# Moving v's copies, two matmul fillers, one group's normalisation and the last value units, and turning a third of batch 4's q by DMA, in a windowed-attention and gated-MLP kernel

## The chip, the cores and the metric

One core of one Trainium2 chip. The metric is device time in microseconds (us) for one execution of the whole program; the time of a kernel is the median of its runs.

## The reference

Sliding-window causal attention (window 64) over q, k, v of 8 batches, 8 heads, 576 positions and head size 64, and on its output, seen as 4608 tokens of 512 features, a two-layer MLP with the gate h·cos(h):

```python
scores = 1/sqrt(64) * q @ k^T                 # per batch and head
mask   = 0 <= query - key < 64
attn   = softmax(where(mask, scores, -1e9))
x      = (attn @ v) as (B*S, H*D)             # 4608 x 512
h      = x @ w_in                             # 512 -> 2048
out    = (h * cos(h)) @ w_out                 # 2048 -> 512, float32
```

## The kernel before, in words

**Units and groups.** Queries are cut into blocks of 64 positions (j = 0 to 8 in each batch) and heads into pairs p = 0 to 3. A *unit* is one (batch, pair, block): a 128 x 128 score tile that holds two heads over 64 queries, and the 128 keys that the window can reach. Two to four units make a *group*, which passes through the engines as one: scores on PE (`g_scores`), masked maximum on DVE (`g_max`), exponential with row sums on ACT (`g_exp`), reciprocal of the sums on DVE (`g_inv`), multiplication on POOL into the bf16 weights w (`g_norm`; a few on DVE), and a transposition of the weights (`g_trans`): by a DMA that SyncE's queue SP issues ("wT<-w"), or for a few "direct" groups by PE, with a copy on DVE (`g_put`). Then `values` multiplies the turned weights with v on PE, eight units for each pair, and `put_x` copies the result from PSUM into xT.

Groups are numbered: 0 to 7 are blocks 0 to 7 of batch 0 and 8 its block 8. Of batch 1, group 9 + 2p has blocks 0 to 3 of pair p, 10 + 2p blocks 4 to 6, and 17 and 18 the rest. `n_listed` is 19, so groups 19 to 28 are batch 2: 19, 20, 22, 23 are blocks 0 to 3 of one pair each, 21 has blocks 4 and 5 of pairs 0 and 1, and 24, the sixth, those of pairs 2 and 3; 25 to 28 have blocks 6 to 8. Batch 3 has six groups of 3, 3, 4, 3, 3, 4 units for blocks 0 to 4, and four of 4 units for blocks 5 to 8.

**v.** v's rows are loaded 128 to a chunk into every other slot of a tile. A block's keys may straddle two chunks, so the odd slots are filled by copies within the tile, one for each half of the partitions (`spread_v`): by a DMA from SP, or by POOL or DVE.

**q and k.** From batch 2 on they arrive in six chunks of 96 positions. k's chunks are turned by DMA transposes from SP (`turn_k`). q is turned by PE, six small transposes for each pair (`tr_q`), which DVE copies into the block layout qB (`put_block`). For the batches named in `TURNED`, the first 2 chunks (batches 5 and 6), or all 6 (batch 7), are turned by DMA instead (`turn_q`), and two DVE copies put them in place (`put_turned`).

**The MLP.** Tokens are taken in tiles of 512 (mt = 0 to 8). In one tile's stage PE does 64 matmuls with w_in (line 440), ACT takes the sine of each of the 16 results, DVE multiplies (gT, line 579), and PE does 64 matmuls with w_out (line 590). The scores of the next batch are placed among the second 64, and at the end of the stage come the next tile's values (line 371).

**What sets the order.** The program of each engine is in the order in which the Python code emits it. Up to the values of mt = 1 that is written out by hand in `FIRST` (a list of short codes: `Gn.13.p` is `g_norm` of group 13 on POOL, `y.0.s` is v's copy of batch 1, half 0, by SP, `Gc` a DMA transposition of weights, `V.2` the values of pair 2). After that, steps are entered with planned times (`at`) and emitted by `pump` as the matmuls pass these times; T = 32 is a stage in plan time. An engine runs its instructions in order and waits at the first that is not ready, so a step placed earlier or later on one queue (SP's and POOL's among them) moves all that stands behind it.

Of the kernel before, what the change touches and what calls it, by code (L numbers as in the profile page):

```python
# [10 lines left out]
def _safe_warn(msg, *a, **kw):  # L11
# [3 lines left out]
F32 = mybir.dt.float32  # L15
# [9 lines left out]
NC, NP = 6, 96  # L25
GF = 4
# [11 lines left out]
PAIRS = 4  # L38
Q = 16
T = 2 * Q  # L40
# [1 line left out]
SKEW = 3  # L42
DIRECT = (0, 7, 8)
OUTS = 3
TURNED = {5: 2, 6: 2, 7: 6}

# [24 lines left out]
)  # L71


# [1 line left out]
def kernel(  # L75
# [9 lines left out]
    nc = tc.nc  # L85
    B, H, S, D = q.shape
# [5 lines left out]
    MT = 512  # L92
    TU = MT // 64
# [8 lines left out]
    ps_t = ctx.enter_context(tc.tile_pool(name="ps_t", bufs=3, space=PSUM))  # L102
# [13 lines left out]
    ident = const.tile([128, 128], BF16, name="ident")  # L116
# [5 lines left out]
    st = {}  # L122
# [9 lines left out]
    def bank(which, name):  # L132
        return ps.tile([128, 512], F32, tag=which, name=name)
# [57 lines left out]
    def spread_v(b, half, engine="p", lo=0, hi=4):  # L191
        vt = vtiles[b % 2]
        hi = min(hi, 4 - (half == 0))
        d = slice(64 * half, 64 * half + 64)
        of = 2 * lo + 2 * (half == 0)
        to, of = vt[d, 2 * lo + 1:2 * hi:2], vt[d, of:of + 2 * (hi - lo) - 1:2]
        if engine == "s":
            nc.sync.dma_start(out=to, in_=of)
        else:
            copy(engine, to, of)  # L200
# [80 lines left out]
    def g_scores(n, which):  # L281
        s_ps = bank((BANKS if n < n_listed else S_BANKS)[which], "s_ps")
        units = groups[n]
        s_ps = s_ps[:, 0:len(units) * 128].rearrange("p (u c) -> p u c", c=128)
        if n < n_first:
            m0 = 2 if units[0][2] else 0
            for h in range(2):
                d = slice(64 * h, 64 * h + 64)
                nc.tensor.matmul(out=s_ps[d].rearrange("p u c -> p (u c)"), lhsT=ident[d, d],
                                 rhs=mask16[d, m0:m0 + len(units)].rearrange("p u c -> p (u c)"),  # L290
                                 start=True, stop=False, skip_group_check=True)
        for u, (b, p, j) in enumerate(units):
            kt = st["kT", b, p]
            lo = max(64 * j - 64, 0)
            rhs = kt[:, lo:lo + 128].rearrange("d (a t) -> d a t", a=2)
            if j and j % 2 == 0:
                rhs = rhs[:, ::-1, :]
            if b > 1:
                nc.tensor.matmul(out=s_ps[:, u].rearrange("p (a t) -> p a t", a=2),  # L299
                                 lhsT=qblocks[(b % 2) * PAIRS + p][:, j].rearrange("d h t -> d (h t)"), rhs=rhs,  # L300
                                 start=True, stop=True, skip_group_check=True)
                continue
            for h in range(2):
                d = slice(64 * h, 64 * h + 64)
                nc.tensor.matmul(out=s_ps[d, u].rearrange("p (a t) -> p a t", a=2),  # L305
                                 lhsT=qtiles[b * PAIRS + p][d, 64 * j:64 * j + 64], rhs=rhs[d], start=n >= n_first,
                                 stop=n >= n_first or u == len(units) - 1, skip_group_check=True)
        st["s", n] = s_ps
# [39 lines left out]
    def g_trans(n):  # L348
        w, u = st.pop(("w", n)), len(groups[n])
        if n in direct:  # L350
            st["tw", n] = t_ps = ps_t.tile([128, GF, 128], BF16, tag="t", name="tw_ps")
            for i in range(u):
                nc.tensor.transpose(t_ps[:, i], w[:, i], ident)
            return
        wT = att.tile([128, GF, 128], BF16, tag="wT", name="wT", bufs=20)
        nc.sync.dma_start(out=wT[:, 0:u], in_=w[:, 0:u].rearrange("p u c -> p (u c)"), transpose=True)
        st.update({("wT", unit): wT[:, i] for i, unit in enumerate(groups[n])})
# [4 lines left out]
        st.update({("wT", unit): wT[:, i] for i, unit in enumerate(groups[n])})  # L362


    def values(mt, p):
        st["o", mt, p] = o_ps = bank("S", "o_ps") if mt > 1 and p == PAIRS - 1 else ps_t.tile([128, MT], F32, tag="t", name="o_ps")
        for i in range(TU):
            b, j = divmod(mt * TU + i, NU)
            wT = st["wT", (b, p, j)]
            for h in range(2):  # L370
                nc.tensor.matmul(out=o_ps[64 * h:64 * h + 64, 64 * i:64 * i + 64],  # L371
                                 lhsT=vtiles[b % 2][:, max(j - 1, 0), 128 * p + 64 * h:128 * p + 64 * h + 64],
                                 rhs=wT[:, 64 * h:64 * h + 64], start=True, stop=True, skip_group_check=True)
# [90 lines left out]
    def at(time, fn, *args):  # L464
        plan.append((time, len(plan), fn, args))
# [10 lines left out]
    n = n_listed  # L476
    for t in range(1, B - 1):
        last = max(i for i, units in enumerate(groups) if units[0][0] == t + 1)
        time = T * t + Q - 1.4
        for i in range(last + 1 - n):  # L480
            time += PACE * len(groups[n - 1]) if i else 0
            at(time, g_scores, n, i % 3)
            lags = LAGS[:2] + tuple(T * t + T - 0.79 - time + 0.01 * s for s in range(3)) if n == last else LAGS
            for lag, fn in zip(lags, (g_max, g_exp, g_inv, g_norm)):
                at(time + lag, fn, n)
            at(time + (4.6 if n in direct else lags[-1]), g_trans, n)
            if n in direct:
                at(time + 4.9, g_put, n)
            ready.update({unit: time + (5.9 if n in direct else 8.5) for unit in groups[n]})
            n += 1  # L490

    for b in range(2, B):
        t0 = T * (b - 1)
        for h in range(2):
            if b in TURNED:
                at(t0 + 0.6 + 0.5 * h, put_turned, b, h, 0, 3)
            if TURNED.get(b, 0) > 2:
                at(t0 + (11 + h if TURNED[b] == NC else 10 + 0.5 * h), put_turned, b, h, 3, TURNED[b] * NP // 64)
        for c in range(TURNED.get(b, 0)):
            at(t0 - T + (23.4 if c < 2 else 26.4) + 0.01 * c, turn_q, b, c)  # L500
        for p in range(PAIRS if TURNED.get(b) != NC else 0):
            t_q = t0 + (2 if b == 2 else 1) + (3.3 if b == 2 else 3.5) * p
            for lag, fn, *args in ((0, tr_q), (0.02, put_block, 0), (0.5, put_block, 1)):
                at(t_q + lag, fn, b, p, *args)
        if b > 2:
            for c in range(NC):
                for i, name in enumerate(("q", "k")):
                    at(t0 - T + 5.6 + 1.6 * c + 0.8 * i, load_chunk, name, b, c)
        for c in range(NC):
            at(t0 + (2 + 1.2 * c if b == 2 else (-5.4, -5.3, -5.2, -4, -2.5, -1.5)[c] if TURNED.get(b) == NC else c - 5.5),  # L510
               turn_k, b, c)
        for c in range(5):
            at(t0 + 0.5 + c, load_v, b, c)
        for half_ in range(2):
            at(t0 + (22.2 + 0.1 * half_ if b > 2 else 10), spread_v, b, half_, "p" if b > 2 else "s")
    for mt in range(2, n_mt):
        for p in range(PAIRS):
            time = T * mt - (8.01 if mt == n_mt - 1 else 1.01)
            at(time, values, mt, p)
            at(time + (0.2 if p < 2 else 0.2 + 0.1 * p), put_x, mt, p, "a" if p == 2 else None)  # L520


# [7 lines left out]
    def spread_first(lo, hi):  # L530
        return lambda i, engine: spread_v(0, i, engine, lo, hi)
# [10 lines left out]
             "pq": lambda p, engine: put_q(0, p, engine), "pk": lambda p, engine: put_k(0, p, engine),  # L542
             "Pq": lambda p, engine: put_q(1, p, engine), "Pk": lambda p, engine: put_k(1, p, engine),
             "zA": spread_first(0, 1), "zB": spread_first(1, 3), "zC": lambda engine: spread_v(0, 1, engine, 3, 4),
             "y": lambda half_, engine: spread_v(1, half_, engine),
             "s": lambda p, g, which: g_scores(2 * p + g, which), "m": lambda p, g: g_max(2 * p + g),
             "e": lambda p, g: g_exp(2 * p + g), "i": lambda p, g: g_inv(2 * p + g),
# [82 lines left out]
```

## Time and profile before

| | us |
|---|---|
| runs shown | 518.71, 310.45, 311.47 |
| their median | 311.47 |
| the profiled execution | 311.39 |
| its span on the core | 309.6 |

| engine | busy us | share of the span |
|---|---|---|
| PE (TensorE matmul) | 295.6 | 95% |
| ACT (ScalarE) | 235.8 | 76% |
| DVE (VectorE) | 229.1 | 74% |
| POOL (GpSimd) | 191.9 | 62% |

The profile is of one execution. All times in its views count from the start of its span. A row of a timeline gives start, length, engine, source line, operation, "out<-in" by tile names, how many instructions it merges, and in brackets the idle time of the engine before it with what ended it. A row of the chain of waits gives start, length and what was on the chain. A row of the windows gives the window, its length, and the busy time of each engine with its instruction count, then the granted TensorE clock.

### The profile page before, as it was taken

Reading aid. Unit: us, or ns where it says so; the run is one execution under the profiler, and the core shown is the slowest. Engines: PE = TensorE matmul, PEld = TensorE weight load, DVE = VectorE, ACT = ScalarE, POOL = GpSimd, SP = SyncE. Lnnn points to the kernel's source line nnn. Section 1 sums busy time; section 2 is a strip of 40 time slices with the busy share of each in tenths; the row PEclk is TensorE's granted clock in tenths of the full one; section 3 lists DMA queues with packets and bytes.
Section 4 is the critical chain, followed back from the end, with each engine's and each line's share of the span. In section 5 each row is a group of like instructions: output and inputs, shape, how many; then the busy total and the mean of one; then the engine's idle time right before and its main releaser. Section 6 shows DMA issues by size and latency. Waiting matters only on the chain.

```text
span 309.6 us, 7899 instructions
## 1 busy us (share of the span) xinstructions
PE 295.6 (95%) x2587; PEld 160.3 (52%) x2619; DVE 229.1 (74%) x877; ACT 235.8 (76%) x785; POOL 191.9 (62%) x227
## 2 busy tenths in 40 slices
PE   3889999899999999999999999999999999999996
PEld 3768844445545455455454555455545554454443
DVE  5998988589767986798679876987598758335801
ACT  4998799577997699769976998699869986116600
POOL 8998577993569659966997699858902840000000
PEclk9999999999999999999999999999999999999999
DMA  8999999999949993999999999999993834011011
GB/s 151 179 214 186 200 178 136 132 156 177 242 81 126 143 235 68 105 125 228 146 97 121 193 191 92 149 173 192 120 134 78 197 70 152 2 68 71 0 65 71
DMA packets 159321, 42.14 MB, mean 136 GB/s; under 512 B 147440, under 2 KB 154544, under 8 KB 159280
## 3 DMA queue, kind: packets, MB, share of 16 engines
q0 software_dynamic: 100192, 18.06, 82.6%
q1 hardware_dynamic: 58944, 23.38, 42.0%
q8 instruction: 20, 0.33, 0.5%
q14 instruction: 21, 0.17, 0.2%
q10 hardware_dynamic: 144, 0.20, 0.2%
HBM read 36.70 MB, written 9.44 MB: 149 GB/s over the span
## 4 chain that ended last, share of the span: by engine, by line
PE 77%; DMA 8%; DVE 5%; POOL 3%; ACT 3%; issue 2%; POOLq 0%; DVEq 0%; ACTq 0%
PE h_ps L440 31%; PE out_ps L590 30%; PE h_ps L404 4%; DMA w_in<-in_moe_w_in_dram 3%; PE s_ps L299 3%; DVE gT L579 3%; DMA wT<-w 3%; PE out_ps L423 3%; PE o_ps L371 3%; ACT e L330 3%; DMA q<-in_q_dram 2%; POOL w L344 1%; POOL v L187 1%; PE out_ps L452 1%; PE tq_ps L218 1%
## 5 line engine op out<-in xcount | busy, mean ns | idle before, releaser
L590 PE MATMUL out_ps<-w_out,gT 128*128 128x512 bf16 x482 | 115.3, 379 | 0.8 <-issue 0.2
L440 PE MATMUL h_ps<-xT,w_in 128*128 128x512 bf16 x498 | 114.6, 379 | 1.0
L330 ACT ACTIVATE e<-s,negm 128x128 f32<-128x128 f32 x256 | 98.6, 388 | 0.6 <-DVE negm L319 0.6
L576 ACT ACTIVATE sin<-h_ps 128x512 f32<-128x512 f32 x128 | 73.8, 598 | 33.1 <-PE h_ps L440 31.0
L579 DVE TENSOR_TENSOR gT<-h_ps,sin 128x512 bf16<-128x512 f32 x128 | 82.0, 685 | 22.2 <-ACT sin L576 21.5
L344 POOL TENSOR_TENSOR w<-e,rden 128x512 bf16<-128x512 f32 (+1 forms) x75 | 71.2, 965 | 37.5 <-DVE rden L337 36.3
L440 PEld LDWEIGHTS <-w_in 128*128 128x128 bf16 x512 | 48.8, 98 | 54.7 <-issue 0.4
L590 PEld LDWEIGHTS <-gT 128*128 128x128 bf16 x496 | 46.0, 98 | 44.1
L319 DVE CUSTOM_DVE_ANT_0 s<-s_ps,mask 128x128 f32<-128x128 f32 x256 | 58.5, 286 | 1.3 <-PE s_ps L305 1.0
L330 ACT ACTIVATION_READ_ACCUMULATOR e<-s,negm 128x1 f32 x256 | 48.2, 188 | 0.0
L181 POOL DMA_DIRECT2D k<-in_k_dram x36 | 28.3, 788 | 9.9 <-DMA k<-in_k_dram 7.8
L187 POOL DMA_DIRECT2D v<-in_v_dram x40 | 34.3, 875 | 0.2 <-issue 0.2
L181 POOL DMA_DIRECT2D q<-in_q_dram x36 | 28.6, 794 | 7.1 <-DMA v<-in_v_dram 2.5
L337 DVE RECIPROCAL rden<-den 128x4 f32<-128x4 f32 (+1 forms) x79 | 13.7, 173 | 21.0 <-ACT e L330 18.0
L136 ACT COPY out_sb<-out_ps 128x512 f32<-128x512 f32 (+1 forms) x18 | 10.2, 565 | 24.5 <-PE out_ps L590 18.4
L299 PEld LDWEIGHTS <-qB 128*128 128x128 bf16 x216 | 17.1, 98 | 14.2
L136 DVE CAST xT<-o_ps 128x512 bf16<-128x512 f32 x24 | 15.6, 679 | 10.6 <-PE o_ps L371 10.5
L136 DVE COPY out_sb<-out_ps 128x512 f32<-128x512 f32 x18 | 12.4, 689 | 12.9 <-PE out_ps L590 12.4
L299 PE MATMUL s_ps<-kT,qB 128*128 128x128 bf16 x216 | 21.9, 219 | 0.0
L319 DVE DVE_READ_ACCUMULATOR2_ANT negm<- 128x1 f32 x256 | 21.3, 83 | 0.0
L136 POOL COPY v<-v 64x1536 bf16<-64x1536 bf16 (+1 forms) x10 | 16.8, 1676 | 0.3
L136 DVE COPY qB<-tq_ps 64x576 bf16<-64x576 bf16 (+1 forms) x40 | 16.4, 410 | 0.3
(65 smaller groups left out, 253.6 us busy)
## 6 DMA issues: line engine op xcount, KB each, us to landing
out_dram<-out_sb SPq DMA_DIRECT2D x16, 512.0 KB, 7.6
v<-in_v_dram POOLq DMA_DIRECT2D x32, 128.0 KB, 5.8
q<-in_q_dram POOLq DMA_DIRECT2D x36, 96.0 KB, 8.6
k<-in_k_dram POOLq DMA_DIRECT2D x36, 96.0 KB, 8.6
w_in<-in_moe_w_in_dram POOLq DMA_DIRECT2D x4, 512.0 KB, 9.6
w_out<-in_moe_w_out_dram POOLq DMA_DIRECT2D x4, 512.0 KB, 10.9
wT<-w SPq DMA_TRANSPOSE x68, 4.4
q<-in_q_dram POOLq DMA_DIRECT2D x7, 144.0 KB, 5.5
```

The costliest lines, as they stand in the source:

```text
L136: {"a": nc.scalar.copy, "p": nc.gpsimd.tensor_copy}.get(engine, nc.vector.tensor_copy)(out, in_)
L181: nc.gpsimd.dma_start(out=st[name, b][:, c].rearrange("p (h d) -> p h d", h=H), in_=src.rearrange("h p d -> p h d"))
L187: nc.gpsimd.dma_start(out=vt.rearrange("p (h d) -> p h d", h=H), in_=v[b, :, c * 128:c * 128 + n, :].rearrange("h p d -> p h d"))
L299: nc.tensor.matmul(out=s_ps[:, u].rearrange("p (a t) -> p a t", a=2), lhsT=qblocks[(b % 2) * PAIRS + p][:, j].rearrange("d h t -> d (h t)" ...
L319: nc.vector.tensor_tensor_reduce(out=s[:, u], in0=s_ps[:, u], in1=mask[:, 2 - j % 2 if j else 0], scale=-scale if b else -1.0, scalar=BIG, ...
L330: nc.scalar.activation(e[:, u], s[:, u], AF.Exp, bias=negm[:, u:u + 1], scale=1.0 if n < n_first else -1.0, accum_out=den[:, u:u + 1])
L337: nc.vector.reciprocal(out=rden[:, 0:len(groups[n])], in_=den[:, 0:len(groups[n])])
L344: (nc.gpsimd if engine == "p" else nc.vector).tensor_tensor(out=w[:, 0:u], in0=e[:, 0:u], op=ALU.mult, in1=rden[:, 0:u].unsqueeze(2).to_br ...
L440: nc.tensor.matmul(out=st["h", ff], lhsT=w_in_sb[:, ks, ff * 128:ff * 128 + 128], rhs=st["xT", mt][:, ks], start=start, stop=stop)
L576: nc.scalar.activation(sin, h_ps, AF.Sin, bias=math.pi / 2.0)
L579: nc.vector.tensor_tensor(out=gt[:, e], in0=h_ps, in1=sin, op=ALU.mult)
L590: nc.tensor.matmul(out=o_ps[e], lhsT=gT[ff // 2][:, ff % 2, ms * 128:ms * 128 + 128], rhs=w_out_sb[:, ff], start=ff == 0, stop=ff == n_ff - 1)
```

## The change

- `TURNED` gains batch 4 with 2 chunks: SP issues two DMA transposes of q in the stage before, planned at 24.3 (the other batches have 23.4), which puts them behind the sixth weights of batch 3 on SP's queue. PE's transposes for batch 4 go from 24 to 16; DVE's eight copies from `tr_q` take 6 of 9 blocks each, and two copies from the turned tile are added.
- In `FIRST` v's copy of batch 1, half 0, leaves SP (`y.0.s`, one DMA of 64 x 3 x 512). POOL does it in two parts: `yA.p` (2 x 512) behind the weights of group 14, `yB.p` (512) behind those of group 13.
- Group 24's multiplication goes from POOL to DVE.
- Fillers on PE: one 128 x 512 matmul of the mask ahead of group 12's scores, and four 128 x 128 transposes of the identity ahead of group 6's. Their results are written over.
- v's POOL copies for batch 3 are planned at 24 instead of 22.2. On POOL they move from behind the fourth of batch 3's ten multiplications to behind the sixth.
- For mt = 2 and 3, the values of pairs 2 and 3 are emitted in two steps: units 0 to 5 of both, then units 6 and 7 of both.
- The loads of batch 7's v are planned 7.5 later. On POOL's queue their order is the same as before.

```diff
+FILL = (6, 12)
-TURNED = {5: 2, 6: 2, 7: 6}
+TURNED = {4: 2, 5: 2, 6: 2, 7: 6}
...
-    "Gi.14 Gm.15 Gs.17.1 oc.1.d Gc.9 y.0.s Gn.11.p Gi.13 Gm.16 o.1.2 Ge.8 Ge.16 Ge.15 y.1.d Gn.14.p Gi.8 "
-    "Gc.12 Gm.17 o.0.3.0 Gi.16 Gn.13.p Gc.11 Gn.8.p Lq2.3 Lq2.4 Lq2.5 o.2.2 Gn.16.d Gw.8 Gc.14 Gc.13 "
...
+    "Gi.14 Gm.15 Gs.17.1 oc.1.d Gc.9 Gn.11.p Gi.13 Gm.16 o.1.2 Ge.8 Ge.16 Ge.15 y.1.d Gn.14.p yA.p Gi.8 "
+    "Gc.12 Gm.17 o.0.3.0 Gi.16 Gn.13.p yB.p Gc.11 Gn.8.p Lq2.3 Lq2.4 Lq2.5 o.2.2 Gn.16.d Gw.8 Gc.14 "
...
     def g_scores(n, which):
         s_ps = bank((BANKS if n < n_listed else S_BANKS)[which], "s_ps")
         units = groups[n]
+        if n == FILL[1]:
+            nc.tensor.matmul(out=s_ps, lhsT=ident, rhs=mask16[:, 0:4].rearrange("p u c -> p (u c)"), start=True, stop=True,
+                             skip_group_check=True)
...
             st["tw", n] = t_ps = ps_t.tile([128, GF, 128], BF16, tag="t", name="tw_ps")
+            for i in range(GF if n == FILL[0] else 0):
+                nc.tensor.transpose(t_ps[:, i], ident, ident)
...
-    def values(mt, p):
-        st["o", mt, p] = o_ps = bank("S", "o_ps") if mt > 1 and p == PAIRS - 1 else ps_t.tile([128, MT], F32, tag="t", name="o_ps")
-        for i in range(TU):
+    def values(mt, p, lo=0, hi=TU):
+        if lo == 0:
+            st["o", mt, p] = bank("S", "o_ps") if mt > 1 and p == PAIRS - 1 else ps_t.tile([128, MT], F32, tag="t", name="o_ps")
+        o_ps = st["o", mt, p]
+        for i in range(lo, hi):
...
-            for lag, fn in zip(lags, (g_max, g_exp, g_inv, g_norm)):
+            for lag, fn in zip(lags, (g_max, g_exp, g_inv)):
                 at(time + lag, fn, n)
+            at(time + lags[3], g_norm, n, "d" if n == n_listed + 5 else "p")
...
-            at(t0 - T + (23.4 if c < 2 else 26.4) + 0.01 * c, turn_q, b, c)
+            at(t0 - T + (24.3 if b == 4 else 23.4 if c < 2 else 26.4) + 0.01 * c, turn_q, b, c)
...
-            at(t0 + 0.5 + c, load_v, b, c)
+            at(t0 + (8 if TURNED.get(b) == NC else 0.5) + c, load_v, b, c)
         for half_ in range(2):
-            at(t0 + (22.2 + 0.1 * half_ if b > 2 else 10), spread_v, b, half_, "p" if b > 2 else "s")
+            at(t0 + ((24 if b == 3 else 22.2) + 0.1 * half_ if b > 2 else 10), spread_v, b, half_, "p" if b > 2 else "s")
...
-            at(time, values, mt, p)
+            if mt in (2, 3) and p > 1:
+                at(time, values, mt, p, 0, 6)
+                at(time + 0.001, values, mt, p, 6, TU)
+            else:
+                at(time, values, mt, p)
...
+             "yA": lambda engine: spread_v(1, 0, engine, 0, 2), "yB": lambda engine: spread_v(1, 0, engine, 2, 3),
```

6 rows, old and new, of the table FIRST are left out of this document.

## The prediction

> **What bounds the kernel now.** The page's busy shares put PE first (95% in the table above), so I cut the span into windows at the tiles' stages.
>
> ```profile
> 37.10:59.30 22.20, 20.74 (x263) 10.53 (x267) 17.49 (x76) 18.28 (x80) 16.64 (x21) 1.00 1.65 153
> 59.30:91.80 32.50, 31.55 (x248) 16.44 (x250) 26.30 (x117) 28.45 (x102) 22.09 (x27) 1.00 1.79 164
> 123.70:155.70 32.00, 31.76 (x250) 16.64 (x253) 25.76 (x112) 27.37 (x96) 25.77 (x29) 1.00 1.68 147
> 155.70:187.40 31.70, 31.44 (x243) 16.36 (x246) 25.66 (x114) 27.34 (x96) 26.25 (x30) 1.00 1.79 150
> ```
>
> The number after each window is its length, the next PE's busy time. PE is the bound: in the stages from 123.7 it is busy for all but some 0.25 us of each, so only less PE work shortens them. Two earlier windows leave more: 1.46 us idle in the first row's, 0.95 in the second's. So I asked where in these PE waits, by the chain of waits and PE's timeline.
>
> ```profile
> 51.23 5.50 DMA wT<-w
> 56.77 0.66 PE L371 MATMUL o_ps<-wT,v 128*64 128x64 bf16 x30 [0.94 <-DMA wT<-w]
> ...
> 88.07 3.19 DMA wT<-w
> 91.30 0.51 PE L371 MATMUL o_ps<-wT,v 128*64 128x64 bf16 x20 [0.71 <-DMA wT<-w]
> ```
>
> There are two waits of values for turned weights: 0.94 us at 56.77 (mt = 1) and 0.71 us at 91.30 (mt = 2). The DMAs that end them were issued at 51.23 and 88.07. The whole change can win these 1.65 us and what it takes from PE's work.
>
> **The change part by part.**
>
> *v's copy leaves SP (first wait).* SP, then POOL and DVE, in timelines:
>
> ```profile
> 43.46 2.59 SPq L356 DMA_TRANSPOSE wT<-w  x2
> 46.62 0.60 SPq L198 DMA_DIRECT2D v<-v  x1
> 47.31 15.76 SPq L356 DMA_TRANSPOSE wT<-w  x6
> ...
> 46.72 0.83 POOL L344 TENSOR_TENSOR w<-e,rden 128x384 bf16<-128x384 f32 x1 [0.52 <-PE s_ps L305]
> 48.53 1.04 POOL L344 TENSOR_TENSOR w<-e,rden 128x512 bf16<-128x512 f32 x1 [0.99 <-DVE rden L337]
> 50.48 1.04 POOL L344 TENSOR_TENSOR w<-e,rden 128x512 bf16<-128x512 f32 x1 [0.90 <-DVE rden L337]
> 49.03 1.09 DVE L136 COPY v<-v 64x2048 bf16<-64x2048 bf16 x1
> ```
>
> By the order of the code the transposition at 51.23 is group 13's, whose weights POOL had ready at 48.53 + 1.04 = 49.57. It was late because SP was: the copy of v held the queue from 46.05 (end of the two before it) to 47.31. Without it group 12's goes at about 46.2 (POOL had finished groups 9 to 12 by 46.72 - 0.52 = 46.20), and with 2.59/2 = 1.3 for each, group 13's, the fourth from there, at about 50.1. It landed 5.5 us after issue, at 56.73; from 50.1 even that is 55.6, and PE ran dry at 56.77 - 0.94 = 55.83. So the 0.94 goes.
>
> It costs POOL time. These rows give durations by shape:
>
> ```profile
> L136 POOL COPY v<-v 64x2048 bf16<-64x2048 bf16 x5 | 9.5, 1894 | 0.3
> L136 POOL COPY v<-v 64x1536 bf16<-64x1536 bf16 x5 | 7.3, 1457 | 0.0
> L136 DVE COPY qB<-qT 64x768 bf16<-64x768 bf16 x6 | 2.2, 374 | 0.1
> L136 DVE COPY qB<-qT 64x1536 bf16<-64x1536 bf16 x2 | 1.1, 550 | 0.0
> ```
>
> 512 elements more cost POOL 0.437 us, so yA (1024) takes 1.02 and yB (512) 0.58. yA runs 47.55 to 48.57 in the 0.99 us hole ahead of group 13: 0.04 late. yB would fit the 0.90 us hole ahead of group 8, but for DVE's copy of v. That one should take about 0.67 (374 and 550 ns extended to 2048 elements) and took 1.09, ending 0.55 after POOL's multiplication ended at 49.57: I read that it waited for POOL. Now the two take turns: DVE to 50.2, yB to 50.8, group 8's multiplication 0.3 late; the other way round DVE's reciprocal for group 8 comes at 50.85 and it is 0.5 late; with no quarrel 0. Group 8 is turned by PE itself, and PE was already waiting for it, so this delay reaches PE whole. I take 0.3, the middle, for the waiting copy asked first. Net: -0.94 + 0.3 = **-0.64** (from -0.94 to -0.44).
>
> The Trainium skill, page "SBUF — State Buffer", section "Who interferes with whom", speaks against this move: DVE's copies in the fast modes and GpSimd's instructions lock one port pair for a whole instruction, and the other blocks. The row of 1.09 us agrees. By the rule the delay stays between 0.3 and 0.5; without it the sum would be 0.3 lower.
>
> *Group 24 on DVE, and the last units later (second wait).*
>
> ```profile
> 85.75 2.23 SPq L356 DMA_TRANSPOSE wT<-w  x1
> 86.45 0.18 DVE L337 RECIPROCAL rden<-den 128x4 f32<-128x4 f32 x1 [0.54 <-ACT e L330]
> 86.70 1.04 POOL L344 TENSOR_TENSOR w<-e,rden 128x512 bf16<-128x512 f32 x1 [0.98 <-DVE rden L337]
> L344 DVE TENSOR_TENSOR w<-e,rden 128x512 bf16<-128x512 f32 x3 | 2.1, 689 | 0.1
> 122.59 1.13 PE o_ps L371 x64
> ```
>
> On DVE the weights come at about 86.62 + 0.69 = 87.3 instead of 87.74. But SP was with the transposition before until 87.98, for 2.23 us where 1.3 is usual. If that stays, the gain is 0.1; if it was chance, SP is free at 87.05, and the gain is that of the weights and their place, 88.07 - 87.3 = 0.77. I take 0.25, nearer to what the row shows. DVE's 0.69 pushes the next group's masked maxima and an out copy, for which ACT, a group behind, does not wait. POOL's next multiplications do not come sooner, for they wait for sums.
>
> The split puts 12 matmuls of pair 3 ahead of the late weights: 12 x 1.13/64 = 0.21 of work into the wait. Together **-0.46** (from -0.1 - 0.21 = -0.31 to -0.71, the whole wait). For mt = 3 the row at 122.59 shows 64 matmuls in 1.13 without a wait: nothing there.
>
> *q of batch 4.*
>
> ```profile
> 126.50 0.26 PE tq_ps L218 x6
> L136 DVE COPY qB<-tq_ps 64x576 bf16<-64x576 bf16 x24 | 10.8, 450 | 0.2
> L136 DVE COPY qB<-tq_ps 64x384 bf16<-64x384 bf16 x16 | 5.6, 350 | 0.1
> 111.35 11.84 SPq L356 DMA_TRANSPOSE wT<-w  x7
> 128.53 4.00 SPq L259 DMA_TRANSPOSE kT<-k  x3
> 115.05 3.41 POOL L136 COPY v<-v 64x1536 bf16<-64x1536 bf16 x2
> kT<-k SPq DMA_TRANSPOSE x1, 8.5
> 138.60 0.39 PE L299 MATMUL s_ps<-kT,qB 128*128 128x128 bf16 x4
> ```
>
> PE drops 8 of 24 transposes at 0.26/6: 0.35 us. The same step lies between the windows from 123.7 and from 155.7 (batch 5 has two turned chunks): 31.76 - 31.44 = 0.32. I take **-0.33**. DVE saves 8 x 0.10 and pays 2 x 0.374: even. SP pays two transposes at 4.00/3 = 1.33, and behind them stand the seventh weights and all of batch 4's keys. Their room comes from v's copies: now the fifth weights wait behind 3.41 us of POOL copies, and the seven transpositions take 11.84 us where 7 x 1.33 = 9.3 would do. With the copies behind the sixth weights, these 2.5 us of pause are open to the turns. What the copies hold now is the seventh weights: at the seven's pace (11.84/7 = 1.7 each) the sixth multiplication ends near 115.05 + 2 x 1.7 = 118.4, the copies at 121.9 and the seventh at 122.9, against its issue at 111.35 + 11.84 - 1.2 = 122.0 now: an estimated push of 0.9 on the queue behind. The third chunk of keys, issued at 128.53 and landing 8.5 later at 137.03, is wanted at 138.60: 1.57 of room, of which PE's own 0.33 and the push leave 0.3. Cost 0, but thinly. The copies end ahead of the values at 122.59 too, by 0.7 instead of 4.1.
>
> *Fillers.* One matmul of 512 columns and four transposes of 128: at the 0.26/6 for 96 columns above, 0.23 each.
>
> ```profile
> 17.78 0.35 PE L305 MATMUL s_ps<-kT,qT 64*64 64x128 bf16 x6 [0.51 <-ACT kT L136]
> 18.69 0.40 PE L353 MATMUL tw_ps<-ident,w 128*128 128x128 bf16 x4 [0.23 <-POOL w L344]
> 12.75 10.81 DMA w_in<-in_moe_w_in_dram
> ```
>
> They stand in waits of 0.51 and 0.23 us, and behind both PE waits for w_in's landing at 23.56. Cost 0; without that cover 0.46. Batch 7's loads keep their place on POOL: 0.
>
> **The sum**, against the profiled execution's own 311.39 (span 309.6): 311.39 - 0.64 - 0.46 - 0.33 = **309.96**; that execution is 0.08 under the median of the runs. Own range: 311.39 - 0.94 - 0.71 - 0.35 = 309.4 to 311.39 - 0.44 - 0.31 - 0.32 + 0.46 = 310.8.
>
> **The rivals.**
>
> *A. The first gain runs into the keys of batch 2.* PE comes 0.64 sooner to the first scores of batch 2:
>
> ```profile
> 73.79 0.39 PE L299 MATMUL s_ps<-kT,qB 128*128 128x128 bf16 x4
> 63.25 3.84 SPq L259 DMA_TRANSPOSE kT<-k  x3
> kT<-k SPq DMA_TRANSPOSE x1, 7.7
> ```
>
> The third chunk of its keys, the third of the row at 63.25 (issued at 65.88), lands 7.7 later at 73.58, a margin of 0.2. SP issues it after group 18's weights, which come sooner with PE, so I expect it to move along. Against: 7.7 us is mostly queueing among loads that do not move. If it stays, 0.43 of 0.64 is lost: 310.4.
>
> *B. The sixth group does not do what it says.* SP, not POOL, sets its start: norm 0, only the split's 0.21 and its neighbours: 311.39 - 0.64 - 0.21 - 0.33 = 310.2.
>
> *C. Slower: q's two turns hold up batch 4's keys.* If the turns also push what is behind them on the DMA ring, the third chunk of keys comes late at 138.3 and PE stops there. A turn lands 7.5 us after issue in one later stage, against 4.3 in another (median of two):
>
> ```profile
> qT<-q SPq DMA_TRANSPOSE x1, 7.5
> qT<-q SPq DMA_TRANSPOSE x2, 4.3
> ```
>
> With the 0.9 from above and 2 x 1.33 = 2.7 of ring the chunk lands at 140.6, and PE, which now wants it at 138.3, waits 2.3: 309.96 + 2.3 = 312.3. It decides the sign once the push is over 2.7 us (1.24 of margin and 1.43 of other gains). Against it: the same turns stand ahead of batch 5's and 6's keys, and the rows of these stages show no such wait.
>
> **How the numbers follow.** The forecast 0.50, A 0.20, B 0.13, C 0.12; 0.05 for what I have not seen. Predicted 309.96, given as 310.0. All but C lie between 309.4 and 310.8; runs of one kernel differ by up to 1.0 (310.45 and 311.47), and C reaches 312.3. For 8 in 10 I go from 309.0 to 311.6, which leaves out most of C and little below. A difference of 2% (6.2 us), about what a measurement of this kernel can tell from no change, is beyond every case: faster by more 0.02, within 0.94, slower by more 0.04.
>
> **What would show it.** Right: no wait at PE's values of mt = 1; group 13's transposition issued near 50; group 8's multiplication on POOL 0.3 late or less; the wait at mt = 2 between 0 and 0.5; the stage of mt = 3 shorter by 0.33 and no wait at its first scores. A shows as a wait of scores at about 73.5, C as one at about 137. The forecast is wrong if the values of mt = 1 still wait, if DVE's copy of v and yB put more than 0.5 us ahead of group 8, or if any stage after 92 grows.

## The result, and the profile after

| | before | after |
|---|---|---|
| median of 22 runs each, us | 310.95 | 309.73 |
| lowest and highest | 309.27 to 518.71 | 308.63 to 311.11 |
| the profiled execution | 311.39 | 310.1 |
| its span | 309.6 | 308.3 |

The ratio is 0.9961, with an interval of 0.9946 to 0.9977: 1.2 us less, between 0.7 and 1.7. Ratios are of runs within 1.5% of the fastest of their kernel (the run of 518.71 is out, and in e3 below four of twelve, which its median has in it). By the bound of 2% that is no change, which had the chance of 0.94; 309.73 lies in the range (309.0 to 311.6), 0.27 under the 310.0 that was predicted.

The windows of the profile after (the first is the one with the values of mt = 1 at its end, the others are the stages of mt = 1, 3 and 4, cut at the first matmul with w_in of each):

```profile
36.31:58.53 22.22, 21.63 (x276) 11.46 (x277) 18.29 (x73) 19.00 (x81) 18.11 (x22) 1.00 1.54 152
58.53:90.80 32.27, 31.99 (x254) 16.67 (x254) 26.76 (x120) 28.14 (x102) 22.33 (x28) 1.00 1.85 171
122.79:154.48 31.69, 31.45 (x241) 16.32 (x245) 25.62 (x114) 27.42 (x95) 26.53 (x30) 1.00 1.75 152
154.48:186.13 31.65, 31.41 (x240) 16.30 (x244) 25.59 (x114) 27.24 (x95) 26.14 (x30) 1.00 1.76 151
```

PE's idle time in the first is 22.22 - 21.63 = 0.59, where it was 1.46; in the second 0.28 instead of 0.95. (The prediction's rows begin a little elsewhere in the work. Cut at the same matmuls, from 37.19 to 58.68 to 91.74 before and from 38.10 to 58.53 to 90.80 after, the idle times are the same within 0.01.) The third stage has lost 0.31 of busy time and is as long as the fourth now. So all three parts of the change show, at their places. Now the rows of each.

The first wait, in timelines of SP, POOL, DVE and PE after:

```profile
43.94 13.89 SPq L362 DMA_TRANSPOSE wT<-w  x7
...
48.40 1.03 POOL L137 COPY v<-v 64x1024 bf16<-64x1024 bf16 x1
49.45 1.04 POOL L348 TENSOR_TENSOR w<-e,rden 128x512 bf16<-128x512 f32 x1
50.43 1.07 POOL L137 COPY v<-v 64x512 bf16<-64x512 bf16 x1
51.47 1.03 POOL L348 TENSOR_TENSOR w<-e,rden 128x512 bf16<-128x512 f32 x1
...
49.94 1.09 DVE L137 COPY v<-v 64x2048 bf16<-64x2048 bf16 x1
...
52.56 0.40 PE L359 MATMUL tw_ps<-ident,w 128*128 128x128 bf16 x4 [0.17 <-POOL w L348]
...
56.34 0.95 PE L379 MATMUL o_ps<-wT,v 128*64 128x64 bf16 x48
```

SP's seven transpositions stand in one row with no copy between them, and the 48 matmuls of the values run in one piece: the wait of 0.94 is gone. yA took 1.03 (1.02 had been worked out), and group 13's multiplication follows it at once. yB took 1.07 where its shape alone gives 0.58, beside DVE's copy from 49.94 to 51.03, which itself took its 1.09 again. So the two do take turns, but PE's wait for group 8 in the last row but one is only 0.17 long.

The second wait and q's turns, in timelines of DVE, SP, POOL and PE after:

```profile
86.51 0.69 DVE L348 TENSOR_TENSOR w<-e,rden 128x512 bf16<-128x512 f32 x1
84.13 4.52 SPq L362 DMA_TRANSPOSE wT<-w  x3
89.57 1.20 PE L379 MATMUL o_ps<-wT,v 128*64 128x64 bf16 x64
...
116.99 3.41 POOL L137 COPY v<-v 64x1536 bf16<-64x1536 bf16 x2
119.38 2.51 SPq L244 DMA_TRANSPOSE qT<-q  x2
128.81 3.92 SPq L260 DMA_TRANSPOSE kT<-k  x3
137.29 0.43 PE L303 MATMUL s_ps<-kT,qB 128*128 128x128 bf16 x4
```

DVE has group 24's weights ready at 87.20, SP turns them as the last of its three in 4.52, and the 64 matmuls at 89.57 have no wait in them. With v's copies at 116.99, behind the sixth weights, the turns fit into SP's queue at 119.38, and the third chunk of keys is issued at 128.81, against 128.53 before. PE's four scores that need it took 0.43 where they took 0.39: the chunk landed (by the trace, at 137.46) just as PE asked for it.

And one place where after was worse, though nothing ahead of it was changed. PE's timeline at the start, before and then after:

```profile
13.61 0.28 PE L215 MATMUL tk_ps<-ident,k 64*64 64x64 bf16 x7 [0.77 <-issue]
21.28 1.96 PE L404 MATMUL h_ps<-xT,w_in 128*128 128x256 bf16 x16
```

```profile
14.40 0.28 PE L216 MATMUL tk_ps<-ident,k 64*64 64x64 bf16 x7 [1.63 <-issue]
22.10 1.91 PE L412 MATMUL h_ps<-xT,w_in 128*128 128x256 bf16 x16
```

The transposes of a pair's keys came 0.8 later in this execution, and so did the first matmul of the MLP ("MoE" in the names; 22.10 against 21.28). The fillers lie between the two rows and did not add to it: from one row to the other it is 7.67 before and 7.70 after. In the runs below, where, fillers apart, nothing of this differs, it lies between 21.2 and 21.7 eight times and at 22.2 and 22.4 twice; e1 and e7 have a reason of their own.

The difference between the two profiles, by PE's milestones: first MoE matmul +0.82, from there to the stage of mt = 1 -0.97, that stage -0.79, mt = 2 -0.02, mt = 3 -0.30, the rest -0.05: -1.31, which is the difference of the spans.

### The profile page after: what moved, and what is told of

Same layout as the page of the kernel before. It is cut to its first block, busy times and chain, and to the rows that moved or that the text cites. A ratio compares the mean times of both kernels' runs of the same rounds, so it can differ in the third digit from the quotient of the medians.

```text
span 308.3 us, 7893 instructions
## 1 busy us (share of the span) xinstructions
PE 294.8 (96%) x2584; PEld 159.5 (52%) x2616; DVE 229.8 (75%) x880; ACT 235.9 (77%) x785; POOL 192.6 (62%) x228
## 4 chain that ended last, share of the span: by engine, by line
PE 89%; DVE 3%; ACT 2%; DMA 2%; issue 2%; POOL 1%; DVEq 0%; POOLq 0%; ACTq 0%
PE h_ps L448 35%; PE out_ps L604 34%; PE s_ps L303 4%; PE h_ps L412 4%; PE out_ps L431 3%; PE o_ps L379 3%; DMA k<-in_k_dram 2%; PE tq_ps L219 1%; PE out_ps L460 1%; PE s_ps L309 1%; ACT e L334 1%; PE tk_ps L216 1%; DVE negm L319 1%; DVE v L137 1%; DVE s L323 1%
## 5 line engine op out<-in xcount | busy, mean ns | idle before, releaser
L348 POOL TENSOR_TENSOR w<-e,rden 128x512 bf16<-128x512 f32 (+1 forms) x74 | 70.0, 962 | 34.8 <-DVE rden L341 33.7
L323 DVE DVE_READ_ACCUMULATOR2_ANT negm<- 128x1 f32 x256 | 21.2, 83 | 0.0
L137 POOL COPY v<-v 64x1536 bf16<-64x1536 bf16 (+3 forms) x12 | 18.8, 1570 | 0.3
L137 DVE COPY qB<-tq_ps 64x384 bf16<-64x384 bf16 (+1 forms) x40 | 15.6, 390 | 0.4
```

The costliest lines, as they stand in the source:

```text
L137: {"a": nc.scalar.copy, "p": nc.gpsimd.tensor_copy}.get(engine, nc.vector.tensor_copy)(out, in_)
L323: nc.vector.tensor_tensor_reduce(out=s[:, u], in0=s_ps[:, u], in1=mask[:, 2 - j % 2 if j else 0], scale=-scale if b else -1.0, scalar=BIG, ...
L348: (nc.gpsimd if engine == "p" else nc.vector).tensor_tensor(out=w[:, 0:u], in0=e[:, 0:u], op=ALU.mult, in1=rden[:, 0:u].unsqueeze(2).to_br ...
```

## The experiments

Two questions. Are the waits that the change removes there in every execution of the kernel before? And which of the parts do it? e1 to e4, e5 to e8 and e9 to e12 ran together, each four beside the same 35 runs of the kernel before.

| run | median us | ratio to before, interval |
|---|---|---|
| e1_no_fillers | 309.83 | 0.9958, 0.9926 to 0.9989 |
| e2_v_alone | 310.64 | 0.9996, 0.9968 to 1.0024 |
| e3_keys_first | 313.44 | 1.0039, 1.0000 to 1.0079 |
| e4_six_alone | 310.63 | 1.0000, 0.9966 to 1.0034 |
| e5_before_again | 310.42 | 0.9983, 0.9954 to 1.0011 |
| e6_after_again | 309.86 | 0.9976, 0.9949 to 1.0003 |
| e7_turn_alone | 310.79 | 1.0012, 0.9984 to 1.0039 |
| e8_without_turn | 310.02 | 0.9973, 0.9948 to 0.9998 |
| e9_more_turns | 312.03 | 1.0067, 1.0039 to 1.0095 |
| e10_v_not_moved | 311.39 | 1.0031, 1.0004 to 1.0057 |
| e11_fillers_alone | 310.78 | 1.0008, 0.9983 to 1.0034 |
| e12_24_on_pool | 309.76 | 0.9981, 0.9959 to 1.0003 |

e5 is the kernel before itself, and its ratio is 0.9983, 0.5 us from 1, in an interval of 0.9 us to either side. No part alone had been given more than that, so the traces have to decide.

**The two kernels once more (e5, e6).** No edit.

> The kernel before once more, for a second profile and as a null comparison. Two runs with one part each showed no wait at all in the other part's place (no wait at 55.6 with group 13's transposition issued as late as before; none at 90.4 with POOL doing group 24). Theory 'chance': the two waits of the profile before are late landings that only some executions have; this profile shows none of them, or one, and the first matmul of mt = 2's MLP comes 31.2 to 33 us after that of mt = 1 as chance has it. Theory 'sum': both waits are there again (1.1 at the values of mt = 1, 0.7 to 0.9 at those of mt = 2). Time the same as before.

> The changed kernel once more. Both theories: no wait at the values of mt = 1 and 2, stages 32.26 and 31.99, that of mt = 3 31.67; the start (first matmul with w_in) between 21.2 and 22.5; 1.2 us under the kernel before.

PE's timeline of the kernel before in this second profile:

```profile
57.33 0.66 PE L371 MATMUL o_ps<-wT,v 128*64 128x64 bf16 x30 [1.71 <-DMA wT<-w]
```

The first wait is 1.71 here, not 0.94. The second is not there; another of its kind is, 0.53 at 187.54, at the values of mt = 5. e6 has neither, its stages are 32.26, 31.99 and 31.66 as in the profile after, and its first MoE matmul is at 21.45: the late start of the profile after was that execution's own. So the two waits are landings that come late in some executions. By its ratio e6 is 0.7 us under the kernel before (from 1.6 under to 0.1 over), less than the 1.2 of the first measurement, and within what the two intervals allow.

**v alone (e2), the sixth group alone (e4).** Each part put into the kernel before.

```diff
e2:
-    ... Gc.9 y.0.s Gn.11.p ... Gn.14.p Gi.8 ... Gn.13.p Gc.11 ...
+    ... Gc.9 Gn.11.p ... Gn.14.p yA.p Gi.8 ... Gn.13.p yB.p Gc.11 ...
e4:
+            at(time + lags[3], g_norm, n, "d" if n == n_listed + 5 else "p")
+            if mt in (2, 3) and p > 1:   # values in two steps
```

> The kernel before with one part: v's copy for batch 1 by POOL (yA, yB) instead of SP. Theory 'sum': no wait at the values of mt = 1, PE is at the first scores of batch 2 some 1.0 us sooner (at 72.8 if the start is as early as before), the wait at the values of mt = 2 stays at 0.7, total -1.0. Rival 'keys' (A of the prediction): the third chunk of batch 2's keys lands at 73.4 to 73.6 whatever PE does, so with an early start PE waits there for 0.5 to 0.8 us, and the total falls by 0.2 to 0.5 only.

> The kernel before with one part: group 24's multiplication on DVE, and the values' units 6 and 7 of pairs 2 and 3 last. Theory 'sum': the wait of 0.71 at the values of mt = 2 goes (its transposition is issued 0.5 sooner and lands 1.2 sooner), the stage of mt = 1 is 0.8 shorter, total -0.8. Rival B of the prediction: SP is the limit, the wait shrinks by the split's 0.21 only, total -0.2.

SP and PE at the values of mt = 1 and POOL, SP and PE at those of mt = 2, from timelines of e2; then SP and PE at mt = 1 from those of e4:

```profile
42.65 8.19 SPq L356 DMA_TRANSPOSE wT<-w  x6
55.41 0.95 PE L371 MATMUL o_ps<-wT,v 128*64 128x64 bf16 x48
...
85.63 1.04 POOL L344 TENSOR_TENSOR w<-e,rden 128x512 bf16<-128x512 f32 x1 [0.98 <-DVE rden L337]
81.67 6.30 SPq L356 DMA_TRANSPOSE wT<-w  x4
88.64 1.20 PE L371 MATMUL o_ps<-wT,v 128*64 128x64 bf16 x64
```

```profile
46.94 5.14 SPq L356 DMA_TRANSPOSE wT<-w  x4
55.39 0.95 PE L373 MATMUL o_ps<-wT,v 128*64 128x64 bf16 x48
```

e2, with SP's six in one row, has no wait at mt = 1, but none at mt = 2 either, with group 24 still on POOL and no split. e4 has none at mt = 2, but none at mt = 1 either, though v's copy is on SP and the four transpositions start behind it, at 46.94. Group 13's transposition is issued at 50.87 in e4, 51.56 in e5 and 51.23 in the profile before; it landed 2.9, 5.7 and 5.5 us later. In the profile after it was issued at 50.54 and took 2.5.

What tells these landings apart stands on POOL's queue, which issues loads of batch 2's q at that time. Group 13's transposition on SP and the first of these loads on POOL, in the profile before and then in e4, from timelines:

```profile
51.23 1.22 SPq L356 DMA_TRANSPOSE wT<-w  x1
51.46 0.82 POOL L181 DMA_DIRECT2D q<-in_q_dram  x1
...
50.87 1.22 SPq L356 DMA_TRANSPOSE wT<-w  x1
51.49 0.82 POOL L181 DMA_DIRECT2D q<-in_q_dram  x1
```

Before, SP's issue ended at 52.45, behind the end of POOL's (52.28). In e4 it ended at 52.09, ahead of POOL's 52.31. All profiles divide in this way:

| profiles | end of SP's issue against the end of POOL's, us | landed after its issue, us | wait |
|---|---|---|---|
| before, e5, e11 (v's copy on SP) | 0.2, 0.7 and 0.1 behind | 5.5, 5.7 and 5.4 | 0.94, 1.71 and 0.77 |
| e4, e7 (v's copy on SP) | 0.2 and 0.3 ahead | 2.9 and 3.3 | none |
| the nine with v's copy on POOL | 1.1 to 1.6 ahead | 2.5 to 3.4 | none |

The three late ones landed within 0.5 us of that load. So with v's copy on SP the transposition and the load run a race that either can win, and the move takes the transposition well ahead of it: counted from the first MoE matmul, SP issues it 1.5 us sooner in the profile after (50.54 - 22.10 against 51.23 - 21.28). This is an order read from the profiles; no run moves the load alone.

e2 also settles rival A: with PE 1.1 earlier (first scores of batch 2 at 72.72 instead of 73.79) the third chunk of keys is issued at 64.78 instead of 65.88 and lands at 72.85 instead of 73.61, and the scores do not wait (0.39 for four, as before). The keys move along, by 0.76.

**Group 24 back on POOL, the rest of the change kept (e12).**

```diff
-            at(time + lags[3], g_norm, n, "d" if n == n_listed + 5 else "p")
+            at(time + lags[3], g_norm, n, "p")
```

> The kernel after, with group 24's multiplication back on POOL: the split of the values and all else stay. The prediction's step (POOL's 1.04 instead of DVE's 0.69 makes the weights 0.4 later, but a late landing of the one before decides): values of mt = 2 wait up to 0.5 in an execution where group 24's transposition lands 3 us or more after its issue, and not at all where it takes 2.5. Rival (only DVE's speed removes the wait): a wait of 0.3 to 0.7 in any case. The time of the kernel after within 0.5 either way.

From timelines of POOL, SP and PE of e12:

```profile
85.44 1.04 POOL L348 TENSOR_TENSOR w<-e,rden 128x512 bf16<-128x512 f32 x1 [0.98 <-DVE rden L341]
81.48 6.22 SPq L362 DMA_TRANSPOSE wT<-w  x4
88.45 1.20 PE L379 MATMUL o_ps<-wT,v 128*64 128x64 bf16 x64
```

No wait, and 309.76 against 309.86 of e6: the rival (only DVE's speed removes it) is out. The fourth transposition of the row, group 24's, goes as soon as POOL is done, for SP did not stall for 2.23 as in the profile before.

Counted over all profiles: with v's copy on SP the first wait is there in 3 of 5 (before 0.94, e5 1.71, e11 0.77; not in e4 and e7), without it in none of 9. The second wait is there in 1 of 5 with group 24 on POOL and no split (before 0.71; not in e2, e5, e7 and e11). With DVE's multiplication or the split it occurs once in 9, in e3, for another reason.

**The turns alone (e7), and everything but the turns (e8).**

```diff
e7: -TURNED = {5: 2, 6: 2, 7: 6}
    +TURNED = {4: 2, 5: 2, 6: 2, 7: 6}   # with its 24.3, and v's copies of batch 3 at 24
e8: the reverse of it in the kernel after
```

> The kernel before with one part: two chunks of batch 4's q by DMA, with v's copies of batch 3 behind the sixth multiplication. Both theories: stage of mt = 3 31.67 instead of 31.99, no wait at the first scores of batch 4, so -0.3. Theory 'chance': the places of the two waits are as in any run of the kernel before, with or without wait. Rival 'most of it': the turns are worth more than PE's 0.33, some 0.8 to 1.2, through what they take from DVE and PE in runs with a late start.

> The changed kernel with batch 4's q turned by PE again and v's copies of batch 3 where they were. Theory 'sum': -1.84 + 0.9 of later start = -0.9 against before. Theory 'chance': the v and group 24 parts take away waits that only some executions have: -0.3 to -0.9. Rival 'most of it': -0.2 or less. Stage of mt = 3: 31.99 in all.

The stage of mt = 3 from the windows, e7 and then e8:

```profile
122.79:154.45 31.66, 31.63 (x245) 16.29 (x245) 25.60 (x114) 27.29 (x95) 26.63 (x30) 1.00 1.63 152
```

```profile
121.94:153.94 32.00, 31.97 (x253) 16.62 (x254) 25.75 (x112) 27.47 (x95) 25.78 (x29) 1.00 1.54 147
```

32.00 without the turns and 31.66 with them: the 0.33 is there in each execution, whole. The two times (+0.4 and -0.8 against before) cannot show it.

**The turns without v's move (e10).** This is the test of rival C: the turns stay, and only v's POOL copies go back to where they were.

```diff
-            at(t0 + ((24 if b == 3 else 22.2) + 0.1 * half_ if b > 2 else 10), spread_v, b, half_, "p" if b > 2 else "s")
+            at(t0 + (22.2 + 0.1 * half_ if b > 2 else 10), spread_v, b, half_, "p" if b > 2 else "s")
```

> The kernel after, with v's POOL copies of batch 3 back at their planned place of 22.2, behind the fourth of the ten multiplications: the two turns of batch 4 stay. The prediction's theory (the move opens SP's room for the turns): the fifth weights come 3.4 later on POOL, the turns and what stands behind them on SP come later, and a wait of up to 1 us shows at the values of mt = 3 or at the first scores of batch 4. Rival (there is room enough on SP without the move): the turns are issued near 119 to 121 all the same, there is no wait, and the stage of mt = 3 stays at 31.7; time as after.

POOL's, SP's and PE's timelines of e10, and then a row of its chain of waits:

```profile
113.81 3.41 POOL L137 COPY v<-v 64x1536 bf16<-64x1536 bf16 x2
110.18 10.46 SPq L362 DMA_TRANSPOSE wT<-w  x6
120.73 2.51 SPq L244 DMA_TRANSPOSE qT<-q  x2
130.18 4.07 SPq L260 DMA_TRANSPOSE kT<-k  x3
137.09 0.33 PE L303 MATMUL s_ps<-kT,qB 128*128 128x128 bf16 x3
139.48 0.22 PE L303 MATMUL s_ps<-kT,qB 128*128 128x128 bf16 x1 [2.06 <-DMA kT<-k]
```

```profile
130.18 9.26 DMA kT<-k
```

Rival C, in full. POOL's copies stand ahead of the fifth weights, the six transpositions need 10.46 (8.90 in the profile after), the turns start 1.35 later, the third chunk of keys is issued 1.37 later at 130.18 and lands 9.26 after that, and the fourth matmul of the scores, which needs it, waits 2.06. The stage is 33.88 long, and the median is 1.6 above that of e12, which ran beside it. What I had left as "thinly" covered was covered by one line of the change.

**Four turned chunks for batches 5 and 6 (e9).** If turns pay 0.33 each time, more should pay more.

```diff
-TURNED = {4: 2, 5: 2, 6: 2, 7: 6}
+TURNED = {4: 2, 5: 4, 6: 4, 7: 6}
```

> The kernel after, with four chunks of q of batches 5 and 6 turned by SP instead of two: eight fewer transposes on PE in each of the two stages. My theory (PE's work sets a stage's length as long as SP's queue has room): the stages of mt = 4 and mt = 5 each 0.30 to 0.35 shorter (about 31.35 instead of 31.67), no wait at the first scores of batches 5 and 6, and a time about 0.6 below the kernel after. Rival, C's mechanism from the prediction with four turns instead of two: the turns hold up SP's queue, keys or turned weights land late, PE waits 1 to 2 us in each of these stages, and the time is 1 to 3 above the kernel after.

The stages of mt = 4 and 5 from the windows of e9, and PE's rows at the first scores of batches 5 and 6:

```profile
153.68:186.32 32.64, 31.44 (x237) 16.01 (x236) 25.58 (x116) 27.79 (x95) 26.53 (x30) 1.00 1.74 154
186.32:218.96 32.64, 31.75 (x236) 15.97 (x236) 25.62 (x116) 27.61 (x95) 26.12 (x29) 1.00 1.72 154
```

```profile
169.34 0.22 PE L303 MATMUL s_ps<-kT,qB 128*128 128x128 bf16 x1 [1.17 <-DMA kT<-k]
201.45 0.22 PE L303 MATMUL s_ps<-kT,qB 128*128 128x128 bf16 x1 [0.64 <-DMA kT<-k]
```

Each stage is 1.0 longer, not 0.33 shorter: rival C again, in two other stages. The third chunk of batch 5's keys goes out at 161.39 by the trace, 7.7 after its stage began (5.9 in the profile after), and lands 7.91 later. At these planned times SP's queue has room for two turned chunks, not for four.

**The keys of batch 2 ahead of group 18's weights (e3).** Three of SP's transpositions of keys moved up in the order, a try at more margin.

```diff
-    "Ge.18 Lk2.4 Gi.18 Gn.18.d Gc.18 Lk2.5 Lv1.4 "
+    "Ge.18 Lk2.4 Gi.18 Gn.18.d tk2.0 tk2.1 tk2.2 Gc.18 Lk2.5 Lv1.4 "
```

> The changed kernel with the transposes of batch 2's key chunks 0 to 2 put ahead of group 18's weights on SP's queue (which waited 3.9 us there for these weights). Both theories: the third chunk is issued near 62 instead of 65.70 and lands by 70 instead of 73.44. Theory 'sum': nothing waits for the keys, total as the changed kernel within 0.3 us. Rival 'keys': the wait for them goes where the start is early, total 0.3 to 0.8 us under the changed kernel on average over runs.

POOL's and PE's timelines of e3:

```profile
71.59 0.78 POOL L182 DMA_DIRECT2D q<-in_q_dram  x1 [2.05 <-DMA v<-in_v_dram]
82.18 5.03 POOL L348 TENSOR_TENSOR w<-e,rden 128x512 bf16<-128x512 f32 x5
92.44 0.32 PE L379 MATMUL o_ps<-wT,v 128*64 128x64 bf16 x8 [1.27 <-DMA wT<-w]
```

The keys land early, the third at 67.83, and it costs more than it brings. POOL's loads for batch 3 wait for earlier landings (2.05 in the first row), they stand ahead of the first multiplication on POOL's queue, and that one comes at 82.18 instead of 78.46. The values of mt = 2 pay for it.

**Without the fillers (e1), and the fillers alone (e11).**

```diff
e1:  -FILL = (6, 12)
     +FILL = (-1, -1)
e11: the kernel before, with FILL and its two uses
```

> The changed kernel without the two fillers. Theory 'sum' (the parts add: first wait -1.05, second wait -0.79, q's turns -0.30, and the 0.87 us later start in the profile after is chance): PE's stages as in the changed kernel, total the same within 0.2 us, and the start of the MLP (first matmul with w_in, 21.28 before, 22.10 after) falls anywhere between 21 and 22.5. Rival 'fillers late': the fillers cost the start up to 0.46 us; without them the first matmul with w_in comes by 21.6 and the total falls by 0.3 to 0.5.

> The kernel before with nothing but the five filler instructions. Theory 1, that of the prediction (they lie in waits and do nothing): the time of the kernel before within 0.3, first MoE matmul at about 21.3 to 22.3, with or without a drop of the granted clock near 19. Theory 2 (they keep the clock up): no drop of the granted clock near 19 in this profile, as in the others with fillers, and a time 0.2 to 0.5 below the kernel before, for the first MoE matmul comes sooner in those executions that would have had the drop.

The stages of e1 are those of the kernel after. But these are its windows around 18.5, and below them those of e6:

```profile
15.10:18.50 3.40, 2.03 (x35) 1.53 (x35) 3.34 (x11) 3.40 (x19) 3.40 (x5) 1.00 1.44 201
18.50:21.90 3.40, 3.40 (x58) 2.48 (x57) 2.93 (x18) 2.65 (x13) 2.41 (x3) 0.50 1.22 217
```

```profile
15.10:18.50 3.40, 2.65 (x47) 1.85 (x41) 3.37 (x10) 3.40 (x18) 3.40 (x5) 1.00 1.43 201
18.50:21.90 3.40, 3.07 (x67) 2.46 (x68) 3.18 (x21) 3.24 (x16) 2.68 (x3) 1.00 1.23 215
```

The last but two is the granted clock: it fell to 0.50 for 3.4 us. e7, also without fillers, has the same from 19.5 to 22.9. Their first MoE matmul is at 22.13 and 22.35. Each timed run carries its mean granted clock, which is 0.994 for the profiled executions of e1 and e7, so a mean of 0.995 or less can be counted as the sign of such a drop. Of the runs of kernels without fillers 54 of 163 have it. Of those with fillers it is 2 of 68: 2 of the 22 of the kernel after, and 0 of the 46 of e6, e8, e11 and e12. (e3, e9 and e10 have fillers and 8 of 34; they also have new waits of over 1 us.) So theory 2 holds as to the clock, though the fillers do not rule the drop out.

The price of a drop can be read from the key transposes (13.61 before and 14.40 after, in the rows above) to the first MoE matmul. With a drop it is 8.79 in e1 (13.34 to 22.13) and 8.72 in e7 (13.63 to 22.35). Without one it is 7.55 to 7.86 in four profiles without fillers and 7.54 to 7.83 in six with them, so in these a drop costs 1.0 to 1.1 us and the fillers nothing. (e3 and e10 fall out of this: no drop, but some 0.4 to 0.6 more than the others, with longer waits for weights or keys in between.) The times agree: the runs of before with such a mean are 1.1 to 1.3 us longer than the others in each of the three groups of 35. One in three of that, less the 2 of 68, makes 0.3 to 0.4 us per run on average, an estimate. No time of a whole kernel shows it: e1 and e6, the kernel after without and with fillers, have medians of 309.83 and 309.86, and e11 (+0.2, from -0.5 to +1.1) neither shows nor excludes it. Its profile has the first wait, 0.77 at 56.66.

The Trainium skill, page "TensorE: Matmul & The Clock Gate", section "What's actually happening", has the gate fall to half rate after an idle window of about 3.4 us that runs freely, whatever the kernel does. The length and the half rate agree with the row. The window ahead of the drop was not idle, though: PE was busy for 2.03 of its 3.40 us (2.06 in e7), and with the fillers for 2.65 of the same 3.40 in e6. Where the limit lies, these runs don't say.

## Why the prediction was right

**v's copy (predicted -0.94 + 0.3 = -0.64).** The mechanism held: SP's pause went, group 13's transposition was issued at 50.54 in an execution that started 0.8 late (about 50.1 had been worked out), and no profile without the copy on SP has the wait. The way to it was in part another. The 5.5 us of the landing were carried over from the profile before, which left 0.2 of room (55.6 against 55.83). But the earlier issue, now ahead of POOL's loads, also landed sooner, 2.5 after it, at 53.03, over 3 us ahead of the values at 56.34. The price of the quarrel between POOL and DVE was the term that was mis-sized: yB and DVE's copy did quarrel, 1.07 instead of 0.58, but yB ended 0.47 after DVE's copy (51.50 against 51.03) where 0.58 was counted, and group 8's multiplication came 2.02 after group 13's (51.47 and 49.45) where it had been 1.95 (50.48 and 48.53): 0.07 later, not 0.3. What I did not see is that the 0.94 is itself a sample: 0.94, 1.71, 0.77, 0 and 0 in five executions, 0.68 on average.

**Group 24 and the split (-0.46).** Between the two profiles the whole wait of 0.71 went, my bound. SP's 2.23 was in part chance, which I had named but did not believe (1.74 in the profile after, 1.2 to 2.2 in the others): the issue came at 87.44 instead of 88.07. It also landed 2.45 after that, where I had kept the 3.19. For the median the step was too high: the wait is in one of five profiles, 0.14 on average. e12 does without DVE's multiplication, and four of the five profiles with neither it nor the split have no wait, so none of these runs shows that either helps. Rival B gave DVE's part nothing and agrees with e12, but its reason, that SP and not POOL sets the start, holds in the profile before; in e2, e5, e7 and e12 SP goes as soon as POOL is done.

**q's turns (-0.33).** Right to 0.03 in each execution: 0.30 to 0.34 (stages of e6, e7, after against before and e8). The step "their room comes from v's copies" is what e10 shows. The push of 0.9 that I added did not come: the seventh weights were issued at 121.98 as against 122.0 before. The margin is still gone, because PE asks 1.3 sooner: 137.46 landed, the scores of 137.29 one matmul longer than four.

**Fillers (0).** As a cost, right; as an effect, the reason was incomplete. They do lie in waits and cost nothing that the profiles show, and for that I took them to do nothing; but they mostly keep the granted clock up in the stretch behind them. By the counts and the profiles that is worth some 0.3 to 0.4 us on average, an estimate, and not resolved in a time.

**The sum.** Of -1.43 the median has -1.2 (0.7 to 1.7), and its repeat e6 -0.7 (1.6 less to 0.1 more). By what the runs showed, per average execution: turns 0.33, first wait 0.68, second 0.14, fillers 0.3 to 0.4, less 0.07: 1.4 to 1.5, of which the two waits rest on five profiles each. The agreement of 309.96 with 309.73, and of the profile's 310.1, is in part luck: between the two profiles terms that were too small by 0.25 and 0.22, and some 0.3 of small waits, stand against a start that came 0.82 later. The four parts alone, e2, e4, e7 and e11, sum to +0.5 by their ratios (-0.0004, 0, 0.0012, 0.0008), with about 1.8 to either side, so that they neither show it nor contradict it.

**The rivals.** A is out (e2). C was real, but not in this kernel: it takes e10's or e9's edit, and then costs 2.06 and twice 1.3 (the wait of 1.0 over the old length and the 0.33 that was to be saved). Of the signs of a wrong forecast none came.

What stays open: why a transposition that is issued just behind a load lands with it, and why group 24's took 3.2 us in the profile before and 2.4 to 3.0 in the others.

## What to carry to other kernels

A wait for a DMA's landing in one profile is a sample: take a second profile of the same kernel before its length goes into a sum, and see which transfers of other queues were issued just ahead of it. Here an issue 1.5 us earlier took away waits of 0.8 to 1.7, and in all 14 profiles the order against one load told whether there was a wait. When work moves to a queue that feeds later work, price the margin of the last transfer behind it; here 1.37 us of delay on SP's queue became 2.06 of PE's wait, and the same turns were a gain or a loss by the place of a copy on another engine. A filler that lies in a wait cost nothing here, but had a use: look at the granted clock in the stretch behind it.

## What I had not expected of the hardware

- The same transposition of 128 x 512 weights (group 13's) landed 2.5 to 3.4 us after its issue where the issue ended ahead of POOL's next load, and 5.4 to 5.7 where it ended behind it, by as little as 0.1 us.
- The granted clock fell to 0.50 for 3.4 us after a stretch in which PE was busy for 2.03 of 3.40 us. By the runs' mean clock that is so in about a third of the executions without fillers.
- POOL's copy of 512 elements took 1.07 instead of 0.58 beside DVE's copy of 2048, and DVE's 1.09, as it did before with a multiplication beside it.
